# Second attention of a two-attention kernel: V in rows of 4096 B, and its quads computed in pairs

## The chip, the cores and the metric

The kernel runs on one core of a Trainium2 chip. The metric is the device time of one execution in microseconds (us). The core has a matrix engine (PE, whose weight loads are listed apart as PEld), a vector engine (DVE), a scalar engine (ACT), a Pool engine (POOL, which here only builds two identity matrices) and a sync engine (SP, which here issues every data transfer). Sixteen DMA engines move the data between HBM and the on-chip memory SBUF. Matmul results go to PSUM, eight banks of 2 KB a partition.

## The reference

Two independent blocks, A and B, each project a query, attend over a cache and project back; their outputs stand side by side. All tensors are bf16.

```python
def _A_ref(x, k_cache, v_cache, wq, wo):      # x (16, 32, 1024), caches (16, 4, 1024, 128)
    q = (x @ wq).reshape(B, Sq, Hq, Dh)        # then transposed to (B, 32 heads, 32, 128)
    k = jnp.repeat(k_cache, rep, axis=1)       # 8 query heads share one cache head
    v = jnp.repeat(v_cache, rep, axis=1)
    p = _softmax(jnp.einsum("bhqd,bhkd->bhqk", q, k) * (Dh ** -0.5), axis=-1)
    o = jnp.einsum("bhqk,bhkd->bhqd", p, v)
    return o(as (B, Sq, Hq * Dh)) @ wo
```

B is the same without the sharing: its caches have 32 heads, (16, 32, 1024, 128), so that K and V of B are 128 MiB each, and K and V of A 16 MiB each. With wq and wo (8 MiB each, for A and for B) the kernel reads 337.64 MB by the page. Every byte of the caches is read once.

## The kernel before

**Units of work.** One "quad" is 128 rows of scores: four (batch, head) pairs by 32 queries, against 1024 keys. A has 128 quads (one batch, four of the eight query heads of a cache head); B has 128 (two batches by two heads). The main loop has 128 steps; each step computes one quad of B (`quadB_all`, L940) and about one of A (`quadA_all`, L958), and the small projections around them. `A_STEPS_FRAC` (L21, 0.97) makes A's quads end a little before B's.

**A quad of B**, in order, with the lines by which the profile names it:
- K arrives by two transfers of 512 KB (L750), in rows of 4096 B: a partition holds 16 consecutive keys of one head, `(hh p) (s d)` with s = 16. DVE transposes each in blocks of 32x32 (L785), KB_sb to KBt_sb.
- Scores (L827): 32 matmuls of 32x32 weights by 512 columns, in four operations of eight. An operation's eight use eight of the PE's sixteen 32x32 sub-arrays: four row groups (`rg`), four column groups (`cg`), two row groups to a column group. They fill two PSUM banks, one of the two score buffers in `ps_s`.
- DVE takes the negative maximum of a row (L837), ACT the exponential with its sum (L850), into `P_sb`.
- PE transposes `P_sb` (L862, "id,P_sb"): four f32 transposes of 128x128, each carrying pairs of bf16, into one bank of `ps_g`; ACT or DVE copies it to `PT_sb` (L526).
- The product with V (L892): 32 matmuls with 128x32 weights, four at a time side by side in the four column groups. V arrives by two transfers of 512 KB (L763), in rows of 2048 B: a partition holds eight consecutive keys of a head, and both heads.
- Reciprocal (L901), normalisation (L908 or L909), a transpose of the 128x128 result (L914) and its copy to OTA_sb or OTB_sb (L526). After four quads, the output projection (L680) and its sum in `acc` (L691, L694).

A quad of A differs in its scores (L806, two matmuls of 512 columns), in PV (L884) and in K, which PE transposes (L776). Query projections are at L598 (A) and L616 (B); B's queries are then transposed (L625) and shuffled (L638) into QR.

**Buffers.** V of B has three slots of two tiles (`NVB_SLOTS`), so six tiles of 512 KB; K of B four tiles (`NKB_SLOTS` = 2, of two) and four more tiles for the transposed K; A's K and V two tiles of 256 KB each. A slot is fixed by the step number.

**Order of the work.** The program is written as a list of operations with what each reads and writes. `list_schedule` (L223) plays it through with a table of costs (`DUR`, L35; `PACKET`, L48) and writes each engine's instructions in the order that comes out. Engines then run this order strictly, waiting on semaphores. That includes SP: a transfer whose buffer isn't yet free holds up every transfer behind it. `MODE_SWITCH` (L28) is the cost the planner puts on PE going from one tile shape to another, and `BANK_RESERVE` keeps PSUM banks for projections.

Of the kernel before, what the change touches and what calls it, by code (L numbers as in the profile page):

```python
# [16 lines left out]
NVB_SLOTS = 3  # L17
NKB_SLOTS = 2
LAZY_PER_STEP = 100
LAZY_DELAY = 4  # L20
A_STEPS_FRAC = 0.97  # L21
# [5 lines left out]
PE_MODE = {"scoresB": 2, "Qshuf": 2, "PVB": 1}  # L27
MODE_SWITCH = 0.05  # L28
LOOK = 0.35
# [6 lines left out]
    "scoresB": (0.216, 0.20), "scoresA": (0.216, 0.20), "PT_trA": (0.49, 0.22), "PT_trB": (0.49, 0.22), "PVA": (0.45, 0.22), "PVB": (0.112, 0.22),  # L36
# [11 lines left out]
PACKET = {"kb_dma": (4096, 0.159), "wq_dma": (1024, 0.046)}  # L48
PACKET_DEFAULT = (2048, 0.084)
# [5 lines left out]
def dma_time(op):  # L55
    size, us = PACKET.get(op.name, PACKET_DEFAULT)
    return op.dur / size * us / 16


class _Op:  # L60
    __slots__ = ("eng", "emit", "deps", "sig", "dma_key", "dma_val", "clock", "name", "needs_sig", "waits", "dur", "t0", "t1", "tag", "prio", "idx", "alts", "step")
# [28 lines left out]
SLOTS = {"bank": 4, "P": 3, "PT": 3, "stat": 6, "O": 2}  # L90
# [15 lines left out]
class Prog:  # L106
# [12 lines left out]
    def add(self, eng, emit, reads=(), writes=(), dma_key=None, name="", dur=None, tag=None, prio=0, wtag=None, rtag=None, claims=()):  # L119
# [7 lines left out]
        if dma_key is None:  # L127
            dur = DUR.get(name, (0.2, 0.1))
        self.specs.append((eng, emit, tuple(reads), tuple(writes), dma_key, name, dur, tag, prio))
# [6 lines left out]
        op.step = self.step  # L136
        op.idx = len(self.ops)
        deps = {}
# [22 lines left out]
        if dma_key is not None:  # L161
            op.dma_key = dma_key
            self.dma_count[dma_key] = self.dma_count.get(dma_key, 0) + 1
            op.dma_val = 16 * self.dma_count[dma_key]
# [58 lines left out]
    def list_schedule(self, lat=0.05, look=LOOK):  # L223
        ops = self.ops
        n = len(ops)
        users = [[] for _ in range(n)]
        ndeps = [0] * n
        for op in ops:
            ndeps[op.idx] = len(op.deps)
            for d in op.deps:  # L230
                users[d.idx].append(op.idx)

# [34 lines left out]
        def slot_time(i):  # L267

            t = 0.0
            for v in acq[i]:  # L270
                idle = [slot_free[v.cls][x] for x in range(SLOTS[v.cls]) if held[v.cls][x] is None]
                keep = sum(k for kind, k in BANK_RESERVE.items() if kind != v.kind and not any(h is not None and h.kind == kind for h in held["bank"])) if v.cls == "bank" else 0
                if len(idle) <= keep:
                    return None
                t = max(t, sorted(idle)[0])
            return t
# [34 lines left out]
        while True:  # L311
# [53 lines left out]
            order.append(best)  # L365
            for u in users[best]:
# [13 lines left out]
        for k in seq:  # L380
            eng, emit, reads, writes, dma_key, name, dur, tag, prio = self.specs[order[k]]
            if eng == "any":
                eng = chosen[order[k]]
                name = name + "@" + eng
            newp.add(eng, emit, actual(reads), actual(writes), dma_key, name, dur, tag, prio)
# [45 lines left out]
def build(nc, pa, pb, out):  # L431
# [15 lines left out]
    NVB = NVB_SLOTS  # L447
    NKB = NKB_SLOTS
# [17 lines left out]
    with stack:  # L466
# [7 lines left out]
        zeros = sb("zeros", [P, P], BF)  # L474
        id32 = sb("id32", [P, P], F32)
        z32 = sb("z32", [P, P], F32)
# [4 lines left out]
        Qtok = sb("Qtok", [P, 2, NG, CW], BF)  # L481
# [7 lines left out]
        KB_sb = sb("KB_sb", [P, 2 * NKB, 16 * Dh], BF)  # L489
        KBt_sb = sb("KBt_sb", [P, 2, 2, 16 * Dh], BF)  # L490
        VB_sb = sb("VB_sb", [P, NVB, 2, 2, NCH, Dh], BF)
# [16 lines left out]
        if HOOK is not None:  # L508
            print("sbuf bytes remaining per partition:", nc.sbuf_bytes_remaining() if callable(nc.sbuf_bytes_remaining) else nc.sbuf_bytes_remaining)

        pr.add("pool", lambda g: g.memset(zeros[:], 0.0), writes=["zeros"], name="c0")
        pr.add("pool", lambda g: g.affine_select(ident[:], zeros[:], [[1, P]], ALU.not_equal, 1.0, base=0, channel_multiplier=-1),
               reads=["zeros"], writes=["ident"], name="c1")
        pr.add("pool", lambda g: g.memset(z32[:], 0.0), writes=["z32"], name="c0")
        pr.add("pool", lambda g: g.affine_select(id32[:], z32[:], [[1, P]], ALU.not_equal, 1.0, base=0, channel_multiplier=-1),
               reads=["z32"], writes=["id32"], name="c1")
# [89 lines left out]

        def qprojB(m_, G):
# [3 lines left out]
            v = Virt("bank", "pj")  # L611
            for j0 in range(0, DJ, JS):
                def e_qp(e, j0=j0):
# [5 lines left out]
                pr.add("pe", e_qp, reads=[("wq", 1, k_) for k_ in pcs] + [("xT", 1, G)], writes=[v], claims=[("Qtok", m_ % 2, G)], name="qprojB", dur=0.225 * JS,  # L619
                       rtag=dict((("wq", 1, k_), m_) for k_ in pcs))  # L620
            evac(Qtok[:, m_ % 2, G, :], lambda: bank(v)[:, 0:CW], reads=[], writes=[v, ("Qtok", m_ % 2, G)], name="qB_ev",
                 wtag={("Qtok", m_ % 2, G): m_}, mul=scale)

        def qprepB_tr(m_, G):
            pr.add("dve", lambda e: e.transpose(QBt[:, :].bitcast(F32), Qtok[:, m_ % 2, G, :].bitcast(F32)),  # L625
                   reads=[("Qtok", m_ % 2, G)], writes=["QBt"], name="QBt_tr", rtag={("Qtok", m_ % 2, G): m_}, wtag={"QBt": (m_, G)})
# [39 lines left out]
        def oproj(pi, blk, G):  # L666
# [7 lines left out]
            for oh in range(NOH):  # L674
                v = Virt("bank", "pj")
                for h0_ in range(0, nh, 2):
                    def e_op(e, oh=oh, h0_=h0_, v=v):
                        last = None
                        for hh in range(h0_, h0_ + 2):
                            last = e.matmul(bank(v)[:, 0:OUTW], OT[:, gp, hh, :], wo_[:, hh, oh * OUTW:(oh + 1) * OUTW],  # L680
# [39 lines left out]
        def mk_quadB(t):  # L720
# [10 lines left out]
            q.kvslot = t % 2  # L731
            q.krslot = t % NKB
            q.vslot = t % NVB
            q.first_of_group = (jb == 0)
# [5 lines left out]
        def st_dmaK(q, t_=None):  # L740
            if q.pi == 0:
                if not q.kv_new:
                    return
                sl = q.kvslot
                pr.add("sp", lambda e: e.dma_start(KA_sb[:, sl, :, :], pa["k"][q.b, q.s].rearrange("(p c) d -> p c d", c=NCH)),
                       writes=[("KA", sl)], dma_key=f"ka{sl}", name="ka_dma", dur=Sk * Dh * 2, wtag={("KA", sl): q.kid})
            else:
                sl = (2 * q.t + t_) % (2 * NKB)
                ksrc = pb["k"][q.b0 + t_, q.h0:q.h0 + 2].rearrange("hh (p s) d -> (hh p) (s d)", s=16)
                pr.add("sp", lambda e: e.dma_start(KB_sb[:, sl, :], ksrc), writes=[("KB", sl)], dma_key=f"kb{sl}", name="kb_dma", dur=2 * Sk * Dh * 2, wtag={("KB", sl): q.kid})  # L750

        def st_dmaV(q):
            if q.pi == 0:
                if not q.kv_new:
                    return
                sl = q.kvslot
                pr.add("sp", lambda e: e.dma_start(VA_sb[:, sl, :, :], pa["v"][q.b, q.s].rearrange("(p c) d -> p c d", c=NCH)),
                       writes=[("VA", sl)], dma_key=f"va{sl}", name="va_dma", dur=Sk * Dh * 2, wtag={("VA", sl): q.kid})
            else:
                sl = q.vslot  # L760
                for t_ in range(2):
                    vsrc = pb["v"][q.b0 + t_, q.h0:q.h0 + 2].rearrange("hh (p c) d -> p hh c d", c=NCH)
                    pr.add("sp", lambda e, t_=t_, vsrc=vsrc: e.dma_start(VB_sb[:, sl, t_, :, :, :], vsrc), writes=[("VB", sl, t_)],  # L763
                           dma_key=f"vb{sl}_{t_}", name="vb_dma", dur=2 * Sk * Dh * 2, wtag={("VB", sl, t_): q.kid})
# [16 lines left out]

        def st_ktrB(q, t_):
            sl = q.kvslot
            rs = (2 * q.t + t_) % (2 * NKB)
            pr.add("dve", lambda e: e.transpose(KBt_sb[:, sl, t_, :].bitcast(F32), KB_sb[:, rs, :].bitcast(F32)),  # L785
                   reads=[("KB", rs)], writes=[("KBt", sl, t_)], name="KBt_tr", rtag={("KB", rs): q.kid}, wtag={("KBt", sl, t_): q.kid})
# [8 lines left out]
        def st_scores(q):  # L795
# [3 lines left out]
            q.vbt, q.vbo = Virt("bank"), Virt("bank")  # L799
            vS = q.vS  # L800
            if q.pi == 0:
                sl = q.kvslot
                qt = QT_sb[:, q.s % 2]

                for u in range(2):
                    pr.add("pe", lambda e, u=u: e.matmul(ps_s[:, vS.idx, u, :], qt[:, q.b, q.hh0:q.hh0 + 4, :].rearrange("p a q -> p (a q)"),  # L806
                                                         KTA_sb[:, sl, u * 512:(u + 1) * 512], start=True, stop=True),
                           reads=[("QT", q.s % 2, q.hh0 + a) for a in range(4)] + [("KTA", sl)], writes=vS.res, name="scoresA", dur=0.225,
                           tag="A%d" % q.t, rtag=dict([(("QT", q.s % 2, q.hh0 + a), q.s) for a in range(4)] + [(("KTA", sl), q.kid)]))
            else:  # L810
                sl = q.kvslot
                gp = (q.m * NG + q.G) % 2

                def e_s(e, fp):
                    last = None
                    if True:
# [308 lines left out]
```

## Time and profile before

| what | value |
|---|---|
| median of 3 runs | 901.42 us (900.02 to 903.91) |
| the profiled execution's own time | 904.35 us |
| its span, first to last instruction | 902.6 us (1.75 us less) |
| PE busy / weight loads busy | 836.3 us / 481.8 us |
| DVE busy | 745.3 us |
| ACT busy | 610.8 us |
| granted PE clock, mean | 0.985 |
| read from HBM / written | 337.64 MB / 2.10 MB |
| matmuls, and as many weight loads | 12,864 |

Busy time is the union of an engine's instructions; as matmuls overlap and their ends are modelled, PE's share says little of how near PE is to its peak. A group of instructions is named by line, engine, operation, and output<-inputs; behind the bar stand its busy time, the mean ns of one, and the idle time of the engine just before them with what ended it. In a name such as "ps_g<-VB_sb,PT_sb" the second input is the one loaded as weights. The queue q1 carries the program's transfers, q8 and q14 the engines' own instructions.

### The profile page before, as it was taken

Reading aid. Unit: us, or ns where it says so; the run is one execution under the profiler, and the core shown is the slowest. Engines: PE = TensorE matmul, PEld = TensorE weight load, DVE = VectorE, ACT = ScalarE, POOL = GpSimd, SP = SyncE. Lnnn points to the kernel's source line nnn. Section 1 sums busy time; section 2 is a strip of 40 time slices with the busy share of each in tenths; the row PEclk is TensorE's granted clock in tenths of the full one; section 3 lists DMA queues with packets and bytes.
Section 4 is the critical chain, followed back from the end, with each engine's and each line's share of the span. In section 5 each row is a group of like instructions: output and inputs, shape, how many; then the busy total and the mean of one; then the engine's idle time right before and its main releaser. Section 6 shows DMA issues by size and latency. Waiting matters only on the chain.

```text
span 902.6 us, 29455 instructions
## 1 busy us (share of the span) xinstructions
PE 836.3 (93%) x12864; PEld 481.8 (53%) x12864; DVE 745.3 (83%) x1057; ACT 610.8 (68%) x1384; POOL 1.1 (0%) x8
## 2 busy tenths in 40 slices
PE   6999999999899999999999998999998988999886
PEld 4365555555555555555545455555555554555453
DVE  0578897888887999689887899878979788798885
ACT  3477886677666776676776466776867666586763
POOL 0000000000000000000000000000000000000000
PEclk9999999999999999999999999999999999999999
DMA  9999999999999999999999999999999999999994
GB/s 325 383 389 393 386 385 392 390 393 383 392 387 389 393 380 388 380 386 376 387 385 391 394 369 389 388 393 370 388 387 391 392 391 367 344 393 393 393 377 170
DMA packets 153984, 341.67 MB, mean 379 GB/s; under 512 B 12544, under 2 KB 28928, under 8 KB 153856
## 3 DMA queue, kind: packets, MB, share of 16 engines
q1 hardware_dynamic: 153856, 339.79, 100.6%
q8 instruction: 102, 1.67, 0.8%
q14 instruction: 26, 0.21, 0.1%
HBM read 337.64 MB, written 2.10 MB: 376 GB/s over the span
## 4 chain that ended last, share of the span: by engine, by line
PE 48%; DMA 23%; DVE 19%; ACT 8%; SPq 1%; issue 1%; ACTq 0%; DVEq 0%
DMA KB_sb<-in_B_k_cache_dram 21%; PE ps_s L827 10%; PE ps_g L862 9%; DVE stat L837 8%; DVE KBt_sb L785 8%; PE ps_g L680 6%; ACT P_sb L850 5%; PE ps_g L892 4%; PE ps_g L598 4%; PE ps_g L884 4%; PE ps_g L616 3%; PE ps_s L806 3%; PE ps_g L776 2%; ACT PT_sb L526 1%; PE ps_g L914 1%
## 5 line engine op out<-in xcount | busy, mean ns | idle before, releaser
L785 DVE STREAM_TRANSPOSE KBt_sb<-KB_sb 128x1024 f32<-128x1024 f32 x256 | 311.8, 1231 | 42.5 <-DMA KB_sb<-in_B_k_cache_dram 40.4
L837 DVE TENSOR_REDUCE stat<-ps_s 128x1 f32<-128x1024 f32 x256 | 304.7, 1209 | 50.7 <-PE ps_s L827 34.3
L850 ACT ACTIVATE P_sb<-ps_s,stat 128x1024 bf16<-128x1024 f32 x256 | 285.8, 1119 | 51.5 <-DVE stat L837 50.0
L862 PE MATMUL ps_g<-id,P_sb 128*128 128x128 f32 x1024 | 177.0, 300 | 13.0 <-ACT P_sb L850 4.7
L862 PEld LDWEIGHTS ps_g<-id,P_sb 128*128 128x128 f32 x1024 | 150.5, 207 | 54.9 <-issue 11.1
L827 PE MATMUL ps_s<-KBt_sb,QR 32*32 32x512 bf16 x4096 | 157.2, 399 | 19.5 <-ACT P_sb L850 10.9
L526 ACT COPY PT_sb<-ps_g 128x512 f32<-128x512 f32 x234 | 134.9, 591 | 59.5 <-PE ps_g L862 58.3
L908 ACT ACTIVATE O_sb<-ps_g,stat 128x128 bf16<-128x128 f32 x199 | 71.4, 370 | 63.0 <-PE ps_g L892 32.4
L806 PE MATMUL ps_s<-KTA_sb,QT_sb 128*128 128x512 bf16 x256 | 91.5, 388 | 6.0 <-ACT P_sb L850 5.6
L827 PEld LDWEIGHTS ps_s<-KBt_sb,QR 32*32 32x32 bf16 x4096 | 49.3, 90 | 81.1 <-ACT P_sb L850 17.8
L892 PE MATMUL ps_g<-VB_sb,PT_sb 128*32 128x128 bf16 x4096 | 91.1, 224 | 1.4 <-ACT PT_sb L526 0.9
L892 PEld LDWEIGHTS ps_g<-VB_sb,PT_sb 128*32 128x32 bf16 x4096 | 60.2, 97 | 48.7 <-issue 29.2
L884 PE MATMUL ps_g<-VA_sb,PT_sb 128*128 128x128 bf16 x1024 | 78.8, 220 | 1.8 <-ACT PT_sb L526 0.7
L884 PEld LDWEIGHTS ps_g<-VA_sb,PT_sb 128*128 128x128 bf16 x1024 | 61.6, 98 | 28.2 <-issue 8.5
L616 PE MATMUL ps_g<-wq_sb,xT_sb 128*128 128x512 bf16 x256 | 71.4, 386 | 2.9 <-DMA wq_sb<-in_B_wq_dram 2.8
L680 PE MATMUL ps_g<-woB_sb,OTB_sb 128*128 128x512 bf16 x256 | 68.7, 381 | 4.4 <-ACT OTB_sb L526 1.8
L598 PE MATMUL ps_g<-xT_sb,wq_sb 128*128 128x512 bf16 x256 | 72.0, 385 | 0.3
L680 PE MATMUL ps_g<-woA_sb,OTA_sb 128*128 128x512 bf16 x256 | 63.0, 380 | 1.3 <-DVE OTA_sb L526 1.0
L914 PE MATMUL ps_g<-ident,O_sb 128*128 128x128 bf16 x256 | 51.8, 224 | 3.0 <-ACT O_sb L908 2.0
L850 ACT ACTIVATION_READ_ACCUMULATOR P_sb<-ps_s,stat 128x1 f32 x256 | 51.8, 202 | 0.0
L526 ACT COPY OTA_sb<-ps_g 128x64 f32<-128x64 f32 x114 | 24.7, 216 | 36.7 <-PE ps_g L914 36.1
L691 DVE TENSOR_TENSOR acc<-acc,ps_g 128x512 f32<-128x512 f32 x64 | 41.2, 675 | 8.1 <-PE ps_g L680 7.6
(41 smaller groups left out, 537.5 us busy)
## 6 DMA issues: line engine op xcount, KB each, us to landing
VB_sb<-in_B_v_cache_dram SPq DMA_DIRECT2D x256, 512.0 KB, 8.1
KB_sb<-in_B_k_cache_dram SPq DMA_DIRECT2D x256, 512.0 KB, 9.2
KA_sb<-in_A_k_cache_dram SPq DMA_DIRECT2D x64, 256.0 KB, 7.7
VA_sb<-in_A_v_cache_dram SPq DMA_DIRECT2D x64, 256.0 KB, 8.1
wq_sb<-in_B_wq_dram SPq DMA_DIRECT2D x32, 256.0 KB, 8.6
wq_sb<-in_A_wq_dram SPq DMA_DIRECT2D x32, 256.0 KB, 8.8
woB_sb<-in_B_wo_dram SPq DMA_DIRECT2D x32, 256.0 KB, 9.2
woA_sb<-in_A_wo_dram SPq DMA_DIRECT2D x32, 256.0 KB, 9.1
```

The source lines that it names most:

```text
L526: return e.copy(dst, src) if hasattr(e, "activation") else e.tensor_copy(dst, src)
L598: last = e.matmul(bank(v)[:, 0:tn], wq_sb[:, 0, j, hc * Dh:(hc + 1) * Dh], xT_sb[:, 0, j, t0:t0 + tn], start=(j == 0), stop=(j == DJ - 1))
L616: last = e.matmul(bank(v)[:, 0:CW], xT_sb[:, 1, j, G * P:(G + 1) * P], wq_sb[:, 1, j, :], start=(j == 0), stop=(j == DJ - 1))
L680: last = e.matmul(bank(v)[:, 0:OUTW], OT[:, gp, hh, :], wo_[:, hh, oh * OUTW:(oh + 1) * OUTW], start=(hh == 0), stop=(hh == nh - 1))
L785: pr.add("dve", lambda e: e.transpose(KBt_sb[:, sl, t_, :].bitcast(F32), KB_sb[:, rs, :].bitcast(F32)), reads=[("KB", rs)], writes=[("KBt" ...
L806: pr.add("pe", lambda e, u=u: e.matmul(ps_s[:, vS.idx, u, :], qt[:, q.b, q.hh0:q.hh0 + 4, :].rearrange("p a q -> p (a q)"), KTA_sb[:, sl, ...
L827: last = e.matmul(ps_s[32 * cg:32 * cg + 32, vS.idx, g2, :].rearrange("p (s j) -> p s j", s=16), lhsT, rhs, start=(fp == 0), stop=(fp == 3 ...
L837: pr.add("dve", lambda e: e.tensor_reduce(stat[:, vst.idx, 0:1], ps_s[:, vS.idx, :, :], AXIS.XY, ALU.max, negate=True), writes=vS.res + [v ...
L850: return e.activation(dst, src, ACTF.Exp, bias=stat[:, vst.idx, 0:1], scale=1.0, accum_out=stat[:, vst.idx, 1:2])
L862: last = e.transpose(bank(vb)[:, m * P:(m + 1) * P], p32[:, m:Sk // 2:NPK], id32[:])
L884: last = e.matmul(bank(vb)[:, 0:Dh], ptc_of(vPT, c, 0, P), VA_sb[:, kvs, c, :], start=(c == 0), stop=(c == NCH - 1))
L892: last = e.matmul(bank(vb)[32 * a:32 * a + 32, 0:Dh], ptc_of(vPT, c, 32 * a, 32 * a + 32), VB_sb[:, kvs, a // 2, a % 2, c, :], start=(c == ...
```

## The change

1. A row of V is now 4096 B: a partition holds 16 consecutive keys of one head (`(hh p) (s d)`, as K has it). A transfer stays at 512 KB.
2. Two quads of B (the same two batches, four heads) are computed together. Scores: four operations of 16 matmuls a pair, in place of two times four of 8, on all sixteen sub-arrays, into both score buffers at once. PV: 64 matmuls a pair with 128x32 weights become 128 with 64x32 weights, eight tiles side by side (two halves of the rows, four column groups), 16 keys of a head at a time from each partition.
3. `P_sb` of B is transposed in bf16, 32 transposes of 64x64 a quad in place of four f32 ones of 128x128. The second quad of a pair has its two heads swapped on the partitions, which the output projection undoes by `hh ^ (hh // 2)`.
4. Buffers of B are no longer fixed by step: the planner deals them out. K has four tiles, transposed K four, V seven (six before).
5. The planner's constants are set anew; A's quads end at 0.92 of the steps (0.97 before); one chunk of B's query projection is moved by a step; two scratch tiles of zeros go.

```diff
-A_STEPS_FRAC = 0.97
+A_STEPS_FRAC = 0.92
-PE_MODE = {"scoresB": 2, "Qshuf": 2, "PVB": 1}
-MODE_SWITCH = 0.05
-LOOK = 0.35
+PE_MODE = {"scoresB": 2, "Qshuf": 2, "PVB": 1, "PT_trB": 3}
+MODE_SWITCH = 0.1
+LOOK = 0.2
...
-SLOTS = {"bank": 4, "P": 3, "PT": 3, "stat": 6, "O": 2}
+SLOTS = {"bank": 4, "P": 3, "PT": 3, "stat": 6, "O": 2, "Qtok": 4, "kb": 4, "KBt": 4, "vb": 7}
+KB_AHEAD = 3
+QPB_FIRST = 1
+VB_AHEAD = 2
...
-        VB_sb = sb("VB_sb", [P, NVB, 2, 2, NCH, Dh], BF)
+        VB_sb = sb("VB_sb", [P, SLOTS["vb"], 16, Dh], BF)
...
-                    vsrc = pb["v"][q.b0 + t_, q.h0:q.h0 + 2].rearrange("hh (p c) d -> p hh c d", c=NCH)
+                return e.dma_start(VB_sb[:, v.idx, :, :].rearrange("p s d -> p (s d)"), src.rearrange("hh (p s) d -> (hh p) (s d)", s=16))
...
+        def st_scoresBB(qs):
+            for q in qs:
+                start_quad(q)
...
+                for t_ in range(2):
+                    for hh in range(2):
+                        for g2 in range(2):
+                            for q in qs:
+                                rg = 2 * hh + g2
+                                cg = 2 * (hh ^ q.hp) + t_
...
+            for fp_ in range(4):
+                pr.add("pe", lambda e, fp_=fp_: e_s(e, fp_), reads=[("QR", gp, 2 * bp), ("QR", gp, 2 * bp + 1)] + [v for q in qs for v in q.vKt],
+                       writes=qs[0].vS.res + qs[1].vS.res, name="scoresB", tag="B%d" % qs[0].t,
...
+            def e_ptB(e):
+                for s_ in range(16):
+                    for hh in range(2):
+                        x = 64 * (hh ^ q.hp)
+                        last = e.transpose(bankb(vb)[64 * hh:64 * hh + 64, s_ * 64:s_ * 64 + 64], P_sb[x:x + 64, vP.idx, s_ * 64:s_ * 64 + 64],
+                                           ident[x:x + 64, x:x + 64], tile_position=(x, 64 * hh))
...
+            def e_pv(e, s0):
+                for s_ in range(s0, s0 + 4):
+                    for t_ in range(2):
+                        for hh in range(2):
+                            for q in qs:
+                                c = 2 * (hh ^ q.hp) + t_
+                                w = (2 * s_ + t_) * Sq
+                                last = e.matmul(bank(q.vbo)[32 * c:32 * c + 32, 0:Dh],
+                                                PT_sb[64 * hh:64 * hh + 64, q.vPT.idx, :, :].rearrange("p c q -> p (c q)")[:, w:w + Sq],
+                                                VB_sb[64 * hh:64 * hh + 64, q.vV[t_].idx, s_, :],
+                                                start=(s_ == 0), stop=(s_ == 15), tile_position=(64 * hh, 32 * c))
+            for s0 in range(0, 16, 4):
+                pr.add("pe", lambda e, s0=s0: e_pv(e, s0), reads=[q.vPT for q in qs] + [v for q in qs for v in q.vV], writes=[q.vbo for q in qs],
...
+        def pairB_all(qs):
+            for q in qs:
+                for t_ in range(2):
+                    st_ktrB(q, t_)
+            loadB("kb", qs[1].t + 5)
+            loadB("vb", qs[1].t + 5)
+            st_scoresBB(qs)
+            for q in qs:
+                st_max(q)
+                st_exp(q)
+            for q in qs:
+                st_ptr(q)
+                st_pev(q)
+            st_pvBB(qs)
+            for q in qs:
+                st_recip(q)
+                st_norm(q)
+                st_otr(q)
```

## The prediction

> **What bounds the kernel now.** I read the slices first, then the queues, then stretches of 100 us, then SP's waits, then the chain.
>
> ```profile
> DMA  9999999999999999999999999999999999999994
> GB/s 325 383 389 393 386 385 392 390 393 383 392 387 389 393 380 388 380 386 376 387 385 391 394 369 389 388 393 370 388 387 391 392 391 367 344 393 393 393 377 170
> ...
> q1 hardware_dynamic: 153856, 339.79, 100.6%
> q8 instruction: 102, 1.67, 0.8%
> ...
> PE 48%; DMA 23%; DVE 19%; ACT 8%; SPq 1%; issue 1%; ACTq 0%; DVEq 0%
> ```
>
> The 16 DMA engines are over 90% busy in every slice but the last, and the packets of q1 alone took 100.6% of what 16 engines have in the span (neighbouring packets overlap a little in the records). So the transfers set the pace from about 2 us to 890 us. The chain shows 48% PE, yet that doesn't make PE the bound: the chain passes through whichever engine releases the next buffer. Stretches confirm it:
>
> ```profile
> 400.00:500.00 100.00, 95.31 (x1494) 54.74 (x1478) 85.50 (x124) 70.68 (x163) 0.00 (x0) 1.00 1.04 386
> 700.00:800.00 100.00, 89.05 (x1457) 52.24 (x1457) 84.81 (x123) 66.79 (x152) 0.00 (x0) 0.97 1.01 375
> 890.00:895.00 5.00, 3.59 (x62) 2.74 (x58) 2.08 (x6) 3.70 (x8) 0.00 (x0) 0.68 0.04 12
> ```
>
> Columns: stretch, length, busy us (instructions) of PE, PEld, DVE, ACT, POOL, then clock, DMA share, GB/s. Where the DMA share is 1.04, 386 GB/s flow; at 1.01, 375. After 890 us nothing flows: that is the tail of computing behind the last load.
>
> How much of the span isn't transfer? From the trace's packet records I counted how many packets of q1 are under way at each moment: none for 9.6 us (nearly all at the two ends), and between 30 and 880 us the shortfall below 16 sums to 11.5 us of all engines. So the middle has only 11.5 us of dry DMA to win or to multiply.
>
> **Part 1, the rows of V.** V of B is 256 transfers of 512 KB: 65,536 packets of 2048 B, which become 32,768 of 4096 B. The trace's records of single packets give both prices on one engine: median 85 ns for 2048 B (92,160 packets), 162 ns for 4096 B (32,768, all of them K of B). So 4096 B cost 170 ns in two packets and 162 in one; 8 ns x 32,768 / 16 engines = **16.4 us less**. By the means (88.8 and 165.1, which hold the stalls) it would be 25.7 us. A fit of packet counts to 5 us stretches with full queues gives 85.9 and 163.1 ns, so 17.8 us; I take the medians. The transfers' count, bytes and SP issues (784) stay; one SP issue takes 0.47 us for V and 0.43 us for K, no difference on a queue that issues one every 1.2 us.
>
> The Trainium skill, "DMA: Bandwidth & Descriptors", section "Bandwidth", speaks against any gain: it has loads from HBM bound at about 358 GB/s on the HBM side. The slices show 393 GB/s held, so this trace doesn't agree; by the rule the sum of this part would be nothing.
>
> **Part 2, more instructions to fetch.** PE's matmuls: the transposes of B go from 512 to 128 x 32 = 4096, PV from 4096 to 64 x 128 = 8192, scores stay at 4096 (16 x 4 x 64). That is +7,680 matmuls and as many weight loads, 15,360 instructions. PE now has 25,728 of them and q8 moved 1.67 MB, 65 B each, in 102 packets; so +1.0 MB or +61 packets. At the queue's own share (0.8% of 902.6 = 7.2 us for 102) **+4.3 us**; at the plain byte rate (1.0 MB at 390 GB/s) +2.6 us. I take 4. They go through the same 16 engines, so they lie on the path. Parts 1 and 2 together: **-12.4 us**.
>
> **Part 3, PE.** It is off the path as long as it stays below the DMA.
>
> ```profile
> L862 PE MATMUL ps_g<-id,P_sb 128*128 128x128 f32 x1024 | 177.0, 300 | 13.0 <-ACT P_sb L850 4.7
> L827 PE MATMUL ps_s<-KBt_sb,QR 32*32 32x512 bf16 x4096 | 157.2, 399 | 19.5 <-ACT P_sb L850 10.9
> L892 PE MATMUL ps_g<-VB_sb,PT_sb 128*32 128x128 bf16 x4096 | 91.1, 224 | 1.4 <-ACT PT_sb L526 0.9
> ```
>
> The means (300, 399, 224 ns) are latencies; the rate is in the starts. In the trace's starts eight L827 matmuls begin 1 to 6 ns apart and the next eight 216 ns on: 27 ns each, 110.6 us in all. Four of L892 begin 3 ns apart, the next four 56 ns on: 14 ns each, 57.3 us. A bf16 transpose (L776) is 56 ns, an f32 one (L862) 120. Summed so over all lines PE needs 686 us, plus 790 changes of tile shape (128x128 to 128x32 or 32x32 and back) at about 94 ns (a change from L862 to L892 is 214 ns against 120): 74 us. Together 760 of 902.6 us.
>
> - Joint scores: 16 in the 216 ns of eight, **-55 us**, since they use sub-arrays that stood empty. If a full array serialised them, 0.
> - Transposes: not in the trace at 64x64. Half the columns and two tiles side by side: 16 x 28 ns = 0.45 us a quad for 0.48 now, -4 us; without overlap 0.9 us, +53 us; at the 56 ns of L776 each, 1.8 us, +168 us. I take -4: L892 and L827 both show tiles side by side.
> - PV: eight tiles in 56 ns gives 57 us as now; no overlap of the two row halves, +57 us. I take 0, as L827 shows two row groups in one column group under way together.
> - Changes of shape: blocks of B's scores and PV halve, blocks of the new 64x64 shape come in (up to 128, two changes each). Between -15 and +15 us; 0.
>
> So PE falls from 760 to about 700 us; with the joint scores and both of the other tiles' overlaps lost it is 705 + 53 + 57 = 815 us. Either is below some 889 us of DMA; only the worst transposes and the worst PV together (705 + 168 + 57 = 930 us) would make PE the bound.
>
> A rule against this part: the Trainium skill, "TensorE: Matmul & The Clock Gate", section "Back-to-back issue gap", never lets two matmuls start less than about 25 ns apart for small N. By it, an estimate, 8192 PV matmuls would take 205 us and 4096 transposes 102 us, and PE would come to some 890 us, level with the DMA. In the trace L892's starts average 13.3 ns, 3 ns between neighbouring tiles, so for different tiles I go by the trace.
>
> **Part 4, DVE, ACT, PSUM.** Same instructions in the same shapes (L785 1.23 us, L837 1.21, L850 1.12, evacuations 0.59): 0. exp now writes runs of 32 keys rather than whole rows; A's and B's exponentials, with different orders, all lie between 1.11 and 1.20 us, so 0, bounds 0 and +10 us of ACT time, hidden, as ACT is 68% busy.
>
> **Part 5, waits and buffers.**
>
> ```profile
> SPq L763 <- PE ps_g L892: 136.7, 69, 7.4
> SPq L750 <- DVE KBt_sb L785: 115.2, 77, 5.2
> ```
>
> SP waits for V slots until PV has run, and for K slots until DVE has transposed; other transfers stand queued behind it. Landing takes 8 to 9 us, so about 3.2 MB are under way (8.5 us x 379 GB/s) of some 6 MB of buffers; that hides these waits. After the change a pair holds four V tiles until its joint PV ends, and the joint scores wait for four transposes and both score buffers; behind them on PE stand all transposes and PVs of A. The extra V tile (seven) pays part. PE's 55 us less shorten each release. I take -2 us of the 11.5, bounds -7 and +30.
>
> **Part 6, the two ends.** Start as before. Tail: the last V was issued at 885.7 and the last 12 us compute alone. A now ends earlier, leaving B alone at the end, but a pair has one more maximum and exponential in series (2.4 us). 0, bounds -4 and +4.
>
> **Sum** against the profiled execution: 904.35 - 16.4 + 4 - 2 = 890 us; the same -14.4 on the median, 901.42, gives **887 us**.
>
> **Rivals.**
>
> *The gain isn't there* (893 to 904): packets of 4096 B run at the memory's rate, not the engine's. Against it: 162 against 170 ns is measured in the same stream. For it: no slice is over 394 GB/s, and single-packet times overlap by 4%. Then 901.4 + 4 - 2 = 903; half of it, 895. The change not doing what it says (rows still cut at 2048 B) would give the same time; K's records at 4096 B with the same pattern speak against it.
>
> *Lumps* (905 to 930, slower). A pair lasts 14.1 us (902.6 / 64). From the end of joint scores to the end of joint PV I add 1.2 (maximum) + 2 x 1.3 (exponentials with the sum) + 0.5 + 0.6 + 0.9 + some 0.5 of latency = 6.3 us with four V tiles held. Three free tiles are 3 x 1.34 = 4.0 us of transfer (512 KB at 390 GB/s), A's and the weights' share of those 6.3 us is 1.2 us, so 5.2: what is short must come from K, whose four tiles (5.4 us) are freed only as DVE transposes. If DVE does the maxima first, up to 1.1 us a pair runs dry. From 0.2 us a pair (13 us) the gain is gone; at 0.4 us, 26 us, the time is 913. For it: the waits above. Against: DVE has 17% idle and can spread four transposes over 14 us.
>
> *More than the packets* (872 to 882): with PE 55 us lighter half of the dry 11.5 us goes and the tail loses 4 us: 901.4 - 12.4 - 6 - 4 = 879.
>
> **Chances.** Forecast (882 to 893) 0.52; more 0.16; no or half gain 0.18; lumps 0.14. A measurement here can tell about 0.5% from no change, 4.5 us. Faster by more (below 896.9): 0.52 + 0.16 + a third of 0.18 = 0.74; within: 0.12; slower: 0.14. For 8 in 10 the range runs from 875 (half of "more" lies above) to 904 (all of the no-gain case).
>
> **What would show it.** q1 at 121,088 packets, q8 near 163 and 2.7 MB; slices at 393 to 399 GB/s where they were 386 to 393 (rate up 1.4%); L827 still x4096 but its busy time near 100 us or less; a 64*64 transposing group x4096 and PV x8192 with 64*32. Wrong if the slices keep 388 GB/s (no gain), if many slices fall below 370 (lumps), if PE's starts in PV average over 10 ns or in transposes over 25 (no overlap), or if DVE waits longer for K than its 40 us.

## The result and the profile after

The changed kernel takes 1077.67 us (median of four runs, 1070.57 to 1080.41), the one before 901.47: a ratio of 1.194, 95% interval 1.188 to 1.200. Forecast were 887 us, with a range from 875 to 904. The profiled execution took 1070.57 us, with a span of 1068.8 us.

The page of the changed kernel, the same views as shown of before, and PE's granted clock, which was 9 in every slice of the kernel before:

```profile
PEclk9999889898989898999999898898986899898766
DMA  9999789888997989888799998887979889978883
GB/s 341 386 373 334 281 308 322 321 304 320 359 372 278 364 313 335 328 309 335 282 366 348 339 356 298 318 290 301 338 278 342 290 318 363 363 291 322 295 321 119
...
q1 hardware_dynamic: 121088, 339.79, 86.5%
q8 instruction: 162, 2.65, 1.0%
...
PE 56%; DVE 15%; ACT 15%; issue 12%; DMA 1%; SPq 0%; ACTq 0%; DVEq 0%
```

The packets are those forecast (121,088; q8 162), but the DMA engines are no longer full, most slices lie between 280 and 360 GB/s, and the chain no longer runs through transfers: 1% DMA for 23%. The item "issue", an engine that waits for nothing that the profile shows, has 12% for 1%. One stretch of 100 us (columns as in the prediction):

```profile
400.00:500.00 100.00, 79.43 (x1939) 51.22 (x1954) 71.98 (x105) 61.31 (x138) 0.00 (x0) 0.93 0.88 325
```

It had 386 GB/s, and 95.31 us of PE. In 100 us every engine works less than before, PE too. What they wait for, the longest waits of the changed kernel (us in total, times, longest):

```profile
DVE stat L865 <- PE ps_s L855: 166.5, 60, 10.1
ACT O_sb L955 <- PE ps_g L937: 115.8, 41, 8.5
PEld ps_g L937 <- issue: 84.9, 73, 5.0
...
PE ps_g L937 <- issue: 63.0, 28, 4.9
PEld ps_s L855 <- issue: 48.6, 55, 4.2
```

DVE waits for B's scores and ACT for B's PV; PE itself waits in the middle of these operations, up to 5 us, for nothing that the profile shows. In the kernel before, the same item for B's PV never reached more than 0.5 us at a time:

```profile
PEld ps_g L892 <- issue: 29.2, 72, 0.5
```

The timeline of the changed kernel shows one such place (start us, length, engine, line; in brackets the idle time before):

```profile
716.76 1.28 PE L937 MATMUL ps_g<-VB_sb,PT_sb 64*32 64x128 bf16 x124
717.07 2.31 DVE L865 TENSOR_REDUCE stat<-ps_s 128x1 f32<-128x1024 f32 x2
...
722.92 0.24 PE L937 MATMUL ps_g<-VB_sb,PT_sb 64*32 64x128 bf16 x4 [4.88 <-issue]
```

124 matmuls of a pair's PV run in 1.3 us, four are left, and PE stands still for 5 us; all data for them were there. In the trace's packet records a 16 KB packet of q8, PE's instructions, starts at 720.48 and ends at 721.48, and PE goes on at 722.92, 1.44 us later. The packet before it had started at 713.69. **PE had run out of instructions.**

I call a "gap" a stretch of over 0.45 us between the starts of two successive PE instructions that ends 1.2 to 1.62 us behind the end of a q8 packet. Gaps sum to 134 us (65 of them) in the changed kernel and to 4 us in the one before. Chance has a share in such a count: with its window shifted by 2 to 3 us, earlier or later, it finds 7 to 16 us in the changed kernel and 1 to 7 in the one before. In traces that kept every PE instruction, the large stalls stand at the same place again and again: where 193 + 256k instructions are done, the edge of a 16 KB block (57 of the 104 pauses over 1 us in the first kernel of "An order that knows the fetch" below, none of 23 in the kernel before).

### The profile page after: what moved, and what is told of

The parts are those of the page before. It is cut to its first block, busy times and chain, and to the rows that moved or that the text cites. A ratio compares the mean times of both kernels' runs of the same rounds, so it can differ in the third digit from the quotient of the medians.

```text
span 1068.8 us, 44622 instructions
## 1 busy us (share of the span) xinstructions
PE 826.7 (77%) x20381; PEld 525.4 (49%) x20544; DVE 726.7 (68%) x1030; ACT 621.0 (58%) x1411; POOL 1.1 (0%) x8
## 2 busy tenths in 40 slices
DMA packets 121275, 342.65 MB, mean 321 GB/s; under 512 B 12544, under 2 KB 28928, under 8 KB 121088
## 3 DMA queue, kind: packets, MB, share of 16 engines
q1 hardware_dynamic: 121088, 339.79, 86.5%
q8 instruction: 162, 2.65, 1.0%
## 4 chain that ended last, share of the span: by engine, by line
PE 56%; DVE 15%; ACT 15%; issue 12%; DMA 1%; SPq 0%; ACTq 0%; DVEq 0%
PE ps_s L855 9%; ACT P_sb L878 8%; PE ps_g L703 8%; DVE stat L865 8%; PE ps_g L937 7%; PE ps_g L902 6%; DVE KBt_sb L809 5%; PE ps_g L922 5%; PE ps_g L615 4%; PE ps_g L891 4%; PE ps_g L639 4%; PE ps_s L832 3%; ACT PT_sb L543 3%; PE ps_g L961 2%; PE ps_g L799 2%
## 5 line engine op out<-in xcount | busy, mean ns | idle before, releaser
L809 DVE STREAM_TRANSPOSE KBt_sb<-KB_sb 128x1024 f32<-128x1024 f32 x256 | 300.7, 1215 | 6.4 <-PE ps_s L855 4.1
L937 PE MATMUL ps_g<-VB_sb,PT_sb 64*32 64x128 bf16 x8192 | 96.8, 232 | 69.7 <-issue 63.0
L937 PEld LDWEIGHTS ps_g<-VB_sb,PT_sb 64*32 64x32 bf16 x8192 | 80.4, 94 | 92.9 <-issue 84.9
L855 PE MATMUL ps_s<-KBt_sb,QR 32*32 32x512 bf16 x4096 | 95.9, 443 | 33.5 <-issue 28.9
L902 PE MATMUL ps_g<-id,P_sb 128*128 128x128 f32 x512 | 99.3, 324 | 20.8 <-ACT P_sb L878 8.0
L891 PE MATMUL ps_g<-ident,P_sb 64*64 64x64 bf16 x4096 | 87.2, 201 | 15.9 <-ACT P_sb L878 9.4
L891 PEld LDWEIGHTS ps_g<-ident,P_sb 64*64 64x64 bf16 x4096 | 76.3, 116 | 45.4 <-issue 18.4
L902 PEld LDWEIGHTS ps_g<-id,P_sb 128*128 128x128 f32 x512 | 77.9, 211 | 38.0 <-ACT P_sb L878 10.7
L832 PE MATMUL ps_s<-KTA_sb,QT_sb 128*128 128x512 bf16 x196 | 72.1, 418 | 29.2 <-ACT P_sb L878 23.4
L961 PEld LDWEIGHTS ps_g<-ident,O_sb 128*128 128x128 bf16 x256 | 25.7, 105 | 61.3 <-ACT O_sb L955 29.0
```

The costliest lines, as they stand in the source:

```text
L809: op = pr.add("dve", lambda e: e.transpose(KBt_sb[:, vKt.idx, :].bitcast(F32), KB_sb[:, vK.idx, :].bitcast(F32)), reads=[vK], writes=[vKt] ...
L855: last = e.matmul(ps_s[32 * cg:32 * cg + 32, q.vS.idx, g2, :].rearrange("p (s j) -> p s j", s=16), lhsT, rhs, start=(fp == 0), stop=(fp == ...
L891: last = e.transpose(bankb(vb)[64 * hh:64 * hh + 64, s_ * 64:s_ * 64 + 64], P_sb[x:x + 64, vP.idx, s_ * 64:s_ * 64 + 64], ident[x:x + 64, ...
L902: last = e.transpose(bank(vb)[:, m * P:(m + 1) * P], p32[:, m:Sk // 2:NPK], id32[:])
L937: last = e.matmul(bank(q.vbo)[32 * c:32 * c + 32, 0:Dh], PT_sb[64 * hh:64 * hh + 64, q.vPT.idx, :, :].rearrange("p c q -> p (c q)")[:, w:w ...
```

## The experiments

Theory **instructions**: PE's instructions come in blocks of 256, each fetched by one 16 KB transfer among the data; joint PV and bf16 transposes use blocks up faster than they come. Rival **lumps**, from the prediction: pairs hold and wait for too much at once.

### Half the instructions in PV, the same streaming

```diff
-                for s_ in range(s0, s0 + 4):
+                for s_ in range(s0, s0 + 4, 2):
...
-                                last = e.matmul(bank(q.vbo)[32 * c:32 * c + 32, 0:Dh],
+                                last = e.matmul(bank(q.vbo)[32 * c:32 * c + 32, 0:2 * Dh],
...
-                                                VB_sb[64 * hh:64 * hh + 64, q.vV[t_].idx, s_, :],
-                                                start=(s_ == 0), stop=(s_ == 15), tile_position=(64 * hh, 32 * c))
+                                                VB_sb[64 * hh:64 * hh + 64, q.vV[t_].idx, s_:s_ + 2, :].rearrange("p s d -> p (s d)"),
+                                                start=(s_ == 0), stop=(s_ == 14), tile_position=(64 * hh, 32 * c))
```

> The changed kernel with B's PV done in half as many matmuls, each of 256 columns in place of 128 (two groups of keys of V with the weights of the first: PV of B isn't the reference's). PE streams as many columns, the transfers, buffers and joint waits stay; PE gets 8,192 instructions fewer. Theory 'instructions arrive too slowly' (a block of 256 PE instructions can't come faster than every 3.44 us, the least distance between two q8 packets in the changed kernel, and a pair's PV eats a whole block in about 0.9 us): the 60 gaps of PE within one line (120 us) fall to under 40 us, time 900 to 970 us. Rival 'lumps' (joint waits and four V tiles held until the joint PV ends): nothing in that changes, time 1055 to 1085 us.

Measured: 951.86 us (one run; before 901.54 beside it). Its queues and one of its slice lines:

```profile
GB/s 335 384 392 351 384 355 388 399 365 358 355 360 352 372 377 346 398 335 365 356 357 395 402 394 343 397 356 374 387 355 332 365 338 395 359 348 361 308 407 102
q8 instruction: 130, 2.13, 0.9%
```

32 blocks fewer, gaps down from 134 to 45 us, and 126 us of time back (from 1077.67) with every buffer and joint wait in place. "Lumps" can't explain that. PE's own time for fewer matmuls can't either: the distances between starts in B's PV, pauses over 0.4 us left out, sum to 56 us here and to 74 us in the changed kernel, 18 us less.

### Only the transposes thinner

```diff
-            if q.pi:
+            if False:
                 pr.add("pe", e_ptB, reads=[vP, "ident", vPT], writes=[vb], name="PT_trB")
```

> The changed kernel with B's probabilities transposed as before, four f32 transposes of 128x128 a quad in place of 32 bf16 ones of 64x64 (PV of B then isn't the reference's). PE time of a quad's transposes stays near 0.48 us; 7,168 PE instructions fewer, but PV stays as dense. Theory 'instructions': part of the stalls goes, those within PV stay, 990 to 1050 us. Rival 'lumps': 1055 to 1085 us.

Measured: 1052.47 us (one run), gaps 121 us, q8 at 134 packets. Nearly as many blocks fewer as above, but a fifth of the gain (25 us) and just above the 990 to 1050 us expected: taking instructions out where they were less dense helps little; a pair's PV still uses a whole block in about 1 us.

### Rows of 2048 B back, everything else changed

```diff
-  return e.dma_start(VB_sb[:, v.idx, :, :].rearrange("p s d -> p (s d)"), src.rearrange("hh (p s) d -> (hh p) (s d)", s=16))
+  return e.dma_start(VB_sb[:, v.idx, :, :].rearrange("p (hh c) d -> p hh c d", hh=2), src.rearrange("hh (p c) d -> p hh c d", c=NCH))
```

> The changed kernel with V of B read in rows of 2048 B again into the same tiles (the keys then lie on other partitions than the transposed probabilities, so PV of B isn't the reference's). Theory 'instructions': DMA isn't the bound, so the 16 us of packet time that come back cost little, time 1065 to 1095 us, q1 at 153,856 packets. Rival 'lumps': dry DMA sets the pace, so slower packets lengthen every refill, about +16 us or more over 1071 to 1078.

Measured: 1092.45 us (one run), gaps 141 us. By the number alone it tells little apart: both theories allowed it. It says that the rows themselves didn't slow the kernel: without them it takes 15 us more.

### Rows of 4096 B alone, in the kernel before

```diff
-  vsrc = pb["v"][q.b0 + t_, q.h0:q.h0 + 2].rearrange("hh (p c) d -> p hh c d", c=NCH)
+  vsrc = pb["v"][q.b0 + t_, q.h0:q.h0 + 2].rearrange("hh (p s) d -> (hh p) (s d)", s=16)
...
```

> The kernel before with V of B read in rows of 4096 B and nothing else changed (the keys lie on other partitions than the transposed probabilities, so PV of B isn't the reference's). If the packet prices of the prediction hold (8 ns less for 4096 B), -16.4 us: 882 to 889 us. If the slices were at the memory's own rate, no change: 899 to 904 us.

Measured: 892.53 us (four runs), ratio 0.990, interval 0.988 to 0.991, so -9 us: between the two expectations. Slices reach 402 to 407 GB/s, so the 394 of before weren't the most that the memory gives. But the shortfall below 16 packets under way, in the middle of the span, grew from 11.5 to 15.8 us, which covers some 4 of the 7 us that are missing. SP waited 161 us in place of 137 for PV to free V's slots; that buffers came free too late for the faster transfers fits this, and isn't shown further.

### Nearly no data beside the instructions

```diff
+                if q.t >= 4:
+                    small = src.rearrange("hh (p s) d -> (hh p) (s d)", s=16)[:, 0:256]
+                    return e.dma_start(KB_sb[:, v.idx, 0:256] if kind == "kb" else VB_sb[:, v.idx, 0:2, :].rearrange("p s d -> p (s d)"), small)
```

> The changed kernel with all but the first four quads' transfers of B's K and V cut to their first 512 B a partition, so that 252 MB of the 338 MB aren't moved (B then computes on old data; its results aren't the reference's). The order of the instructions stays. If the 3.44 us between two blocks of PE instructions is the fetch's own round trip, the least distance between q8 packets stays at 2.5 us or more and the gaps of PE that end 1.2 to 1.6 us behind a q8 packet still sum to 60 to 134 us. If it is time behind data packets in the 16 DMA engines, the distance falls under 2 us and the gaps under 20 us. Rival 'lumps': with nothing to refill the time falls under 800 us, gaps or not; 'instructions' expects 850 to 960 us with the round trip its own.

Measured: 973.5 us (one run). The waits for B's PV and scores within PE, and the DMA engines' load:

```profile
q1 hardware_dynamic: 121088, 112.25, 37.8%
...
PEld ps_g L940 <- issue: 38.9, 58, 2.7
...
PEld ps_s L858 <- issue: 18.7, 40, 1.4
```

By q1's bytes 228 MB fewer were moved, not 252. Neither reading is met, both are true in part. The least distance of q8 packets stays 3.3 us, so there is a round trip of its own; but the gaps fall from 134 to 50 us, and 973.5 us lie just above the 850 to 960 expected. Where a block came late, the 256 instructions up to it took a median of 3.6 us here, and 6.0 to 6.2 us in kernels that move all the data (three whose traces kept every PE instruction). The packet takes 1.0 to 1.1 us and PE goes on 1.4 us after it in both; what differs is its start, a median of 1.1 us after PE entered the block before here, and 3.6 to 3.8 us with all the data (2.7 to 3.4 us over all blocks, late or not). With two thirds of the data gone the kernel is still 71 us slower than before, 50 of them gaps: "lumps" had expected under 800 us.

### More instructions in the kernel before

```diff
-                            last = e.matmul(bank(vb)[32 * a:32 * a + 32, 0:Dh], ...
+                            for x, n in ([(0, Dh)] if c == 0 else [(0, Dh // 2), (Dh // 2, Dh // 2)]):
+                                last = e.matmul(bank(vb)[32 * a:32 * a + 32, x:x + n], ...
```

> The kernel before with B's PV cut into more matmuls: from the second group of keys on, each of 128 columns is two of 64 (60 in place of 32 a quad, 7,168 PE instructions more in all, 28 more blocks to fetch; the same result). PE streams the same columns. If instructions cost only where they are dense (a block of 256 in under 3.44 us): a quad's PV is 120 instructions in some 0.5 us and blocks still last over 3.5 us nearly everywhere, so 901 to 912 us with gaps under 15 us. If each instruction had a flat price (the 176 us that the changed kernel lost over 15,360 instructions, 11 ns each): about +82 us, 980 us.

Measured: 950.68 us (four runs), ratio 1.054, interval 1.048 to 1.060. Between the two numbers, and a miss for my theory's size: blocks last a median of 6.7 us in this kernel, but with full traffic a late block takes 6 us to come, not 3.44. The waits show the same item as in the changed kernel:

```profile
PEld ps_g L893 <- issue: 50.8, 89, 2.4
...
PE ps_g L893 <- issue: 19.9, 16, 2.3
```

Gaps are 47 us for 4 before, the time is 48 us more. Nothing of the change is in this kernel but a number of PE instructions. The smaller matmuls aren't free for PE itself: the distances between starts in B's PV, pauses over 0.4 us left out, sum to 71 us for 52 before. So at most 19 of the 48 us could be PE's own time.

### An order that knows the fetch

Three kernels with the instructions of the changed one, but a planner in which a PE operation is late when its block is. The first: 256 instructions take 3.44 us at least. The second: the same with `A_STEPS_FRAC` 0.99, `MODE_SWITCH` 0.05, `STEP_US` 2. The third: edges at the true place, 5.0 us a block. The core of the third:

```diff
+FETCH = 5.0
...
+        def fetch_stall(i, st):
+            b, f, n_ = crossing(i)
+            if b is None:
+                return 0.0
+            return max(0.0, block_at[b - 1] + FETCH - (st + f * ops[i].dur[0]))
...
+                        if eng == "pe":
+                            at[i] += fetch_stall(i, at[i])
```

> The changed kernel, its instructions the same, in another order: the planner now also knows that 256 PE instructions in a row can't be done in less than 3.44 us, and puts a dense operation (64 instructions of PV or of a 64x64 transposition) behind others where it would stall. Theory 'instructions': the gaps fall from 134 us to under 50 us, time 920 to 970 us. Rival 'lumps': pairs and slots are as they were, no gain, 1050 us or more.

> As the kernel with the planner that knows the fetch, and three of the planner's constants set back or near to those of before: A's quads end at 0.99 of the steps (more thin instructions to put between the dense ones, to the end), the change of tile shape priced 0.05, the weight of a step 2. 'Instructions': gaps under 45 us, time 900 to 945 us. 'Lumps': 1040 us or more.

> The changed kernel in an order planned with a better rule for the fetch: PE's blocks begin at every 256th instruction (the gaps of the earlier runs all stand at instruction 193 of 256), and a block can't begin sooner than 5.0 us after the one before it (median start of a q8 packet 2.6 us after PE entered the block before, 1.0 us for the packet, 1.4 us until PE goes on). If the bound is a rate, 162 blocks at 5.0 to 5.8 us are 810 to 940 us and order can win the rest: 940 to 1030 us. If the stalls lengthen with traffic whatever the order: 1050 us or more.

Measured: 1100.85 us (one run, gaps 145 us), 1061.53 us (four runs, ratio 1.175, interval 1.171 to 1.178, gaps 119 us) and 1050.59 us (one run, gaps 143 us). All three miss, and each lies where the other expectation, of no gain, had put it; the gaps show that the stalls are still there. Order didn't cure it, and a sum of the blocks offers a reason: at the 6.0 us that a late block takes under traffic, 162 blocks are 972 us, more than the some 889 us that the data need; 102 blocks are 612 us. By this sum it isn't only the bursts of PV. Nor is it the sum alone: 130 blocks are 780 us, and both kernels with 130 blocks took 951 and 952 us. I have no run that separates rate and bursts further. The 5.0 us of the third planner were too few as well: its 2.6 us were the start over all blocks, and the late ones start a microsecond later.

### Fewer data under way

```diff
+        newp.window = 3
...
+            writes = list(writes) + [("window", self.nth % self.window)]
```

> The changed kernel with each transfer waiting until the one issued three before it has landed, so that at most about 1.3 MB of data are under way (some 2.2 MB now). If a block of instructions waits behind the data already queued, q8 packets start sooner (a median under 2 us after PE enters the block before, in place of 2.6 to 3.4) and the gaps fall under 100 us. If it merely shares the DMA engines packet by packet, the gaps stay at 120 to 150 us and the time doesn't fall.

Measured: 1222.84 us (one run), gaps 85 us, mean 281 GB/s. The gaps fell below 100 us, and packets start about 1 us sooner (2.1 us after PE enters the block before, 3.2 in the changed kernel, both counted roughly, by weight loads). That is the way of the first expectation, though not under its 2 us. But the traffic fell too, since three transfers don't keep 16 engines full; whether a block waits behind data already queued or shares the engines packet by packet stays open.

### The pairs without the dense instructions

The changed kernel with V's rows, the f32 transposes and the PV of before, quad by quad, so with 26,000 PE instructions; and then the same with each quad's scores on their own again:

```diff
-            st_scoresBB(qs)
+            for q in qs:
+                st_scoresBB([q])
```

> The changed kernel with V's rows of 2048 B, B's four f32 transposes and its PV of 128x32 weights put back (the same result; 26,000 PE instructions), while the pairs, the joint scores on sixteen sub-arrays, the joint wait for four transposed K tiles, the dealt slots and all of the planner's new constants stay. 'Instructions': gaps behind q8 packets under 10 us, 885 to 905 us. 'Lumps': pairs starve the DMA whatever PE's instructions are, 950 us or more.

> As the kernel with pairs and PE's old, few instructions (922.6 us), but each quad of B has its own scores again, eight matmuls at a time, waiting for its own two K tiles and one score buffer; pairs in the transposes and PV, dealt slots and the planner's constants stay (the same result). If what is left of 'lumps' (20 us over before) is the joint scores' wait (DVE waited 101 us for them, 34 us before), it goes: 893 to 908 us, and DVE waits for B's scores under 60 us. If it is the slots or the planner's constants, 915 to 928 us. PE needs 55 us more in both.

Measured: 922.63 us (four runs, ratio 1.0225, interval 1.0196 to 1.0255) with joint scores, 899.22 us (nine runs, ratio 0.997, interval 0.995 to 0.999) with single ones. The first misses both expectations and lies between them, and its gaps are 18 us for under 10 expected (11 us with single scores; the shifted windows find 1 to 13 and 2 to 9 us, so part of this is chance). The second is as expected. DVE's wait for B's scores: before, with joint scores, with single ones:

```profile
DVE stat L837 <- PE ps_s L827: 34.3, 51, 2.4
```
```profile
DVE stat L865 <- PE ps_s L855: 100.8, 61, 4.3
```
```profile
DVE stat L865 <- PE ps_s L855: 50.4, 56, 2.6
```

"Lumps" is real, then, but small: 23 us, which go with the joint scores. DVE's wait fits their waiting for both score buffers and four transposed K tiles; which of the two counts isn't separated. V's four tiles held until a joint PV ends, the other half of "lumps", are in neither kernel, as both compute PV quad by quad: no run tests them alone. The halved PV holds them too and takes 29 us more than the pairs with thin instructions, with 28 us more of gaps, which leaves little for them. The dealt slots and new constants together cost nothing. The last of these two is, by 0.3%, faster than the kernel before, and the fastest here whose result is the reference's.

## Why the prediction was wrong

**The difference.** From 901.5 to 1077.7 us are 176 us. Pairs with thin instructions account for 20.6 us of them (922.63 against 902.05). The remaining 155 us come with the rows, transposes and PV of the change; the rows alone gave 9 us in the kernel before. That most of them are late instructions is shown by the halved PV (126 us back) and, on its own, by the extra instructions in the kernel before; the quiet queue agrees. For the last 29 us this is argued, from the gaps of 45 us that the halved PV still has. How they split into standing still (134 us of gaps), PE's granted clock (0.897 for 0.985) and buffers released late (dry DMA in the middle: 143 us for 12) isn't measured separately; these overlap.

**Step by step.**
- *Part 1, rows*: the packet price was right (median 162 ns with the rows alone, as forecast, and 159 in the changed kernel), the gain of 16.4 us mis-sized: 9.0 us. Some 4 of the missing 7 us are more dry DMA, which this part didn't count; the rest stays open.
- *Part 2, instructions to fetch*: **the step that failed.** The counts were right (162 packets for 163, 2.65 MB for 2.7). They were priced as load on the DMA engines, 4 us, and nowhere was asked how soon the next block reaches PE. What the runs showed in its place: under full traffic a late block takes 6.0 to 6.2 us, and PE stands still for 134 us at the edges of blocks. The trace of before could have raised the question, though not answered it, as PE never used up a block in less than 5.8 us there: 102 blocks, never two within 5.4 us of each other, against a pair's PV that I myself put at 256 instructions in 0.9 us.
- *Part 3, PE*: tiles do overlap. In the quiet kernel the starts of B's scores average 14 ns (16 in 216 forecast, 13.5), of the transposes 18 ns (14) and of PV 12 ns with stalls and 9 without pauses over 0.4 us (7). The Trainium skill, "TensorE: Matmul & The Clock Gate", section "Back-to-back issue gap", has a least distance of about 25 ns for short matmuls (N up to 64); for tiles in different places these runs don't show it. The sum of PE's work was never the matter, its supply was. (Its worst cases leave out one: without the joint scores' gain the worst transposes alone make 760 + 168 = 928 us, above the DMA. It didn't come to that.)

```profile
L937 PE MATMUL ps_g<-VB_sb,PT_sb 64*32 64x128 bf16 x8192 | 96.8, 232 | 69.7 <-issue 63.0
L855 PE MATMUL ps_s<-KBt_sb,QR 32*32 32x512 bf16 x4096 | 95.9, 443 | 33.5 <-issue 28.9
L891 PE MATMUL ps_g<-ident,P_sb 64*64 64x64 bf16 x4096 | 87.2, 201 | 15.9 <-ACT P_sb L878 9.4
```

Even with that, PE's scores fell as forecast to under 100 us busy (95.9).
- *Part 5 and the rival "lumps"*: priced at 26 us lost for 0.4 us a pair, measured 23 us. That the size held is luck: I sought it in V's slots and in dry DMA, and found it at the joint scores.
- *What would show it wrong*: slices under 370 GB/s came, as named, but I had put them down to lumps alone. The sign named beside it, a longer wait of DVE for K, did not come: it waited 2.1 us for K's transfers, 40.4 before.
- *The rival that decided wasn't in the list.* It would have been: PE's instructions as a stream with a price of its own, 162 blocks at the time a block takes.

## What to carry to other kernels

Before cutting matmuls into smaller tiles, count PE's instructions, two a matmul, in blocks of 256, and set the blocks against the time that they may take: here a late block cost 6 us beside full traffic, so a kernel of 890 us could feed some 145 blocks if they were spread evenly (an estimate: 890 through 6.0 to 6.2), and kernels slowed down already at 130. A wait named "issue" inside one operation, at the same place in every 256 PE instructions, was this stall here. Joining operations of two units to fill the array can cost more than it saves, if the joint one must wait for both inputs and both buffers while PE wasn't the bound.

## What the runs showed of the hardware

PE's instructions arrive in blocks of 256 (16 KB), and a block's packet starts only about when PE enters the block before: in the six traces that kept every PE instruction, no q8 packet started more than 37 instructions ahead of that edge, and stalls came one block later. From there a late block took 3.6 us with a third of the data moving and 6.0 to 6.2 us with all of it (q1's packets at 84 to 97% of the 16 engines' time), of which 1.0 to 1.1 us are the packet and 1.4 us lie between its end and PE's next instruction. The Trainium skill, "Runtime: NRT & Kernel Launch", section "Instruction fetch mechanics", states the blocks of 16 KiB and the fetch of the next while one is executed, which these traces agree with. For PE it gives room for 2048 instructions, and further down, without naming an engine, for two blocks: packets that start only about when PE comes to the block before agree with the two blocks, and don't show room for eight. It also holds the fetch to be mostly hidden: with the 4 us of the kernel before that agrees, with the 134 us of gaps in the changed one it doesn't.
